# The tail of an attention block: when its output products are dealt out, where its turned sums lie, and which pair of the FFN comes second

## The chip, the cores and the metric

One core of one Trainium2 chip runs the whole program. The metric is device time in microseconds for one execution; the median of a few runs is given. Engines are named as in the profile: PE (TensorE), DVE (VectorE), ACT (ScalarE), POOL (GpSimd), SP (SyncE, which only issues transfers here).

## The reference

One sequence of 2048 rows, 576 columns; 32 heads of 18; an FFN of 4608.

```python
# A: x @ wqkv -> q, k, v; scores = q k^T * Dh**-0.5; p = softmax; o = p v; o @ wo
# B: g = x @ w_gate; u = x @ w_up; h = gelu_tanh(g) * u; h @ w_down
h  = x + A(layernorm(x), wqkv, wo)
h2 = h + B(layernorm(h), w_gate, w_up, w_down)      # what is returned
```

## The kernel before

Numbers are carried in pairs of fp16 (a high part and a remainder), so a product of two matrices is a sum of three products. Rows come in 16 tiles of 128, in NB=4 blocks of 512 (TPB=4 tiles each).

**Attention.** Eight groups of four heads by four query blocks give 32 blocks, n=0 to 31 (NS=32); g is the group and qc the query block. A block has 16 steps, kt, one for each tile of keys. In a step, two score products per pair of heads go to PSUM (`scores_pair`, L441), ScalarE takes their exponentials (L443), and one step later `weigh` (L447) multiplies them with the values into `acc`. The softmax needs the maximum over the keys of each query beforehand: a second run of score products (L400) whose maxima VectorE takes from PSUM (L403). This generator, `maxima`, runs 28 units ahead, at 16 units a block, so that it ends at n=30, kt=4. At the start of block n+1, `out_block` copies the sums of block n (L456, ScalarE, at kt=0), turns them by PE (L460) at kt=1, copies again (L462) and divides on GpSimd (L467 to L480), leaving fp16 pairs in `nat16`, the same memory as `nat`.

When all eight groups of a query block are done (n=28 to 31), its rows go through wo. `turn_o(b)` turns the four tiles of block b by a transposing DMA on SP (L538) into `OT`, which lies in region V. `wo_block(b)` then makes, for each of four tiles and two halves of columns, 14 products (L247) and adds x, fetched by a DMA into one of three buffers (L546), on VectorE (L551); row statistics follow (L159, L160), and after four tiles the reciprocal deviation (`rstd_of`, 13 short VectorE instructions).

**Toward the FFN.** The FFN multiplies 2x2 blocks by seven products instead of four (`quad`, seven products of seven matmuls, L889). For that, `pair_rows(p)` joins row tile i of an earlier and a later block: tiles of blocks 0 and 1 for p=0, of 2 and 3 for p=1. It normalises, forms sums and differences on VectorE and GpSimd (L585 to L589), casts them on ScalarE (L593), forms remainders on VectorE (L595, L596), and turns them by DMA on SP (L599) into `XP[p]`: XP[0] lies in region X, XP[1] in V. Weights come in 18 chunks; `split_mat` scales a chunk's gate or up matrix on ScalarE (L660), forms sums on GpSimd (L663, L666, L669), casts on ScalarE (L664, L667, L676, L685), and forms remainders on GpSimd (L673 to L688). The parts of even chunks lie in region A and of odd chunks in region W. `prepare` and `prepare_down` load and split chunk after chunk.

For chunk c and pair p the FFN runs `gate(c, p)` (one quad), `up(c, p)` (one quad, then the product with the gate on VectorE, a cast on ScalarE and a remainder on GpSimd, L932 to L934) and `down(c, p)` (96 matmuls, L247, added into `nat` on VectorE, L952).

**What sets the order.** Side work is written as Python generators. In the attention loop, `fill` holds products to be mixed in, `side` other work; each is advanced ("taken") twice a step, once for each `scores_pair`. In the FFN, `step(cost)` advances a clock in units, and each generator in `sides` goes on when its due time, raised by what it yields (3 if nothing), has come; a product of a quad counts 7 units, one of down 3.

The program has two parts that matter. The attention loop stands under a manual schedule for PE and POOL: their instructions keep the written order, while a compiler pass orders ACT, DVE and SP. The FFN stands under a manual schedule for every engine:

```python
    with tc.manual_schedule(engines={EngineType.PE, EngineType.Pool}):   # attention
...
    with tc.manual_schedule():                                           # FFN
        turn_o(NB - 1)
...
        ga = gate(0, 0, first_gate)
        for _ in wo_block(NB - 1):
            step(5)
        wait_for(1, "g")
        rows1 = begin(pair_rows(1))
        up(0, 0, ga, first_up)
```

There follow down(0,0), gate(0,1), up(0,1), gate(1,0), down(0,1), up(1,0) and so on. In the attention loop the blocks n=29, 30, 31 begin, at kt=1, with turn_o(0), turn_o(1), turn_o(2) and take up wo_block of the same number as `fill` at once, so that its products stand before the rest of the block's scores; prepare(0) and prepare_down(0) are `side` from n=28, kt=2, and pair_rows(0) is `side` from n=31, kt=1.

Of the kernel before, what the change touches and what calls it, by code (L numbers as in the profile page):

```python
# [30 lines left out]
def tile_block(  # L31
# [500 lines left out]

    OT = view(V, 0, (L // P, TB), F16)
    xbs = [view(V, 28544 + 4 * HALF * i, (HALF,)) for i in range(3)]

    def turn_o(b):
        for i in range(TPB):
            nc.sync.dma_start_transpose(OT[:, :, i * P : (i + 1) * P], nat16[:, b * TPB + i])  # L538

    def wo_block(b, each=False):  # L540

        for t in range(b * TPB, (b + 1) * TPB):
            for i in range(2):
                ws = slice(i * HALF, (i + 1) * HALF)
                xb = xbs[(2 * t + i) % 3]
                nc.sync.dma_start(xb, xv[:, t, ws])  # L546
                pt = next(m_ring)
                k = t - b * TPB
                run(accumulate(pt[:, :HALF], products(slice(k * P, (k + 1) * P), oh, ol, ws,
                                                      (OT[:, :NK], OT[:, NK], OT[:, NK + 1 :]))))  # L550
                nc.vector.scalar_tensor_tensor(nat[:, t, ws], pt[:, :HALF], u_o, xb,  # L551
                                               op0=ALU.mult, op1=ALU.add)
# [18 lines left out]
    def pair_rows(p):  # L571

        ys, z = rows[p]
        for v in ys:
            nc.gpsimd.memset(v[:, :, HALF + 64 : 3 * P], 0.0)
        for i in range(TPB):
            t1, t2 = 2 * p * TPB + i, (2 * p + 1) * TPB + i
            a, b = slice(0, HALF), slice(HALF, D)
            for k, t, h in ((6, t1, a), (3, t1, b)):
                nc.scalar.activation(z[:, k], nat[:, t, h], AF.Identity,  # L580
                                     scale=rs[:, t : t + 1], bias=nb[:, t : t + 1])
            normed(z[:, 0], nat[:, t2, b], t2)
            normed(z[:, 2], nat[:, t2, a], t2)
            yield
            nc.vector.tensor_add(z[:, 1], z[:, 6], z[:, 0])  # L585
            nc.gpsimd.tensor_add(z[:, 4], z[:, 6], z[:, 2])
            nc.vector.tensor_add(z[:, 5], z[:, 3], z[:, 0])
            nc.gpsimd.tensor_sub(z[:, 2], z[:, 2], z[:, 0])
            nc.vector.tensor_sub(z[:, 3], z[:, 3], z[:, 6])  # L589
            for j, k0, k1 in ((1, KA, 7), (0, 0, KA)):  # L590
                y, zz = ys[j], z[:, k0:k1]
                yield 5
                nc.scalar.copy(y[:, :, :HALF], zz)  # L593
                yield 5
                nc.vector.tensor_sub(y[:, :, 3 * P :], zz[:, :, : 2 * P], y[:, :, : 2 * P])  # L595
                nc.vector.tensor_sub(y[:, :, HALF : HALF + 32], zz[:, :, 2 * P :],  # L596
                                     y[:, :, 2 * P : HALF])
                nc.scalar.copy(y[:, :, HALF + 32 : HALF + 64], y[:, :, 2 * P : HALF])
# [3 lines left out]
            yield  # L602

# [34 lines left out]
    g1, _ = stage(W, 17920)  # L638
    sums1 = view(W, 8960, (3, 3, P), F32)
    sumsn = view(W, 28672, (3, 3, P), F32)  # L640
# [184 lines left out]
    def prepare_down(c):  # L825

        def after(k, last):
            while c and ghost[k] < last:
                yield

        if c == 1:
            yield from after("rows", 1)
        load_down(dn if c else d0, c, nc.sync)
        yield 48
        yield from after("d", 2 * (c - 1))
        yield from split_down(dn if c else d0, c)
        kept[c, "d"] = True
# [141 lines left out]
    side = iter(())  # L979
    with tc.manual_schedule(engines={EngineType.PE, EngineType.Pool}):  # L980
        for b in range(NB):
# [11 lines left out]
        for n in range(NS):  # L993
            g, qc = divmod(n, NB)
            acc = singles[3]
            for kt in range(NT):
                take(mxs)
                for pr in range(2):
                    scores_pair(n, kt, pr)
                    if g < NG - 1 or kt >= NT // 4:  # L1000
                        take(fill)
                    take(side)
                take(mxs)
                if prev is not None:
                    weigh(*prev)
# [28 lines left out]
        weigh(*prev)  # L1034
        for _ in out_block(prev[0], prev[2]):
            pass
        run(side)
        run(fill)
    with tc.manual_schedule():
# [19 lines left out]

        prev = (0, 0)  # L1060
        for c in range(NCH):
            for p in range(NPR):
                if (c, p) == (0, 0):
                    continue
                if (c, p) == (0, 1):
                    down(*prev)
                    while rows1 in sides:
                        step(1)
                    ghost["rows"] = 1
                wait_for(c, "g")  # L1070
                ga = gate(c, p)
                if (c, p) != (0, 1):
                    wait_for(prev[0], "d")
                    down(*prev)
                wait_for(c, "u")
# [29 lines left out]
```

## Time and profile before

| | |
|---|---|
| median of 3 runs | 2880.33 us (2877.4 to 2880.98) |
| profiled execution | 2879.98 us, span 2877.7 us |
| PE busy | 2686.3 us, 93% of the span |
| DVE busy | 2253.1 us, 78% |
| ACT busy | 1711.7 us, 59% |
| POOL busy | 1208.6 us, 42% |
| HBM | 40 GB/s over the span |

A row of the timeline reads: start, length, engine, line, operation, output from input, shapes, count; in brackets the idle time of the engine before it and what ended that. "x14" with a length is a run of fourteen. PEld is the load of weights into PE, SPq and POOLq are DMA issues. A row of the chain reads start, length, what.

### The profile page before, as it was taken

The numbers are of one execution on the slowest core, as the hardware profiler recorded it, in microseconds if no ns is written. First come the engines' busy times: TensorE is split into PE (matmuls) and PEld (weight loads), VectorE is DVE, ScalarE is ACT, GpSimd is POOL, SyncE is SP. The second block draws the span as 40 slices with busy tenths as digits, with TensorE's granted clock in tenths as the row PEclk, the third lists the DMA queues.
The fourth block names the chain that finished last, engine by engine and source line by source line (L and its number), as shares of the span: only waits on it lengthen the run. The fifth ranks groups of instructions, "written<-read, shape, count | busy, mean of one in ns | idle before, by whom it ended". The sixth has DMA issues, their size and how long they took to land.

```text
span 2877.7 us, 44734 instructions
## 1 busy us (share of the span) xinstructions
PE 2686.3 (93%) x16822; PEld 1122.5 (39%) x16822; DVE 2253.1 (78%) x3873; ACT 1711.7 (59%) x2144; POOL 1208.6 (42%) x1498
## 2 busy tenths in 40 slices
PE   6999899999999998999887869999999999999999
PEld 3532222222222222222132435555555555555555
DVE  7569899999999999999783477766667666667666
ACT  5217888888888888888766634444344444344431
POOL 0002475576557641121312336545544545555431
PEclk9999999999999999999899989999999999999999
DMA  8121221211212110000011641111111111111101
GB/s 216 55 74 46 73 66 43 63 63 34 59 51 75 59 32 13 1 26 3 5 34 42 124 87 39 42 31 31 31 41 40 31 31 31 31 35 38 31 1 66
DMA packets 146761, 136.27 MB, mean 47 GB/s; under 512 B 84720, under 2 KB 125808, under 8 KB 145392
## 3 DMA queue, kind: packets, MB, share of 16 engines
q1 hardware_dynamic: 134512, 92.99, 12.2%
q0 software_dynamic: 12032, 40.42, 4.4%
q8 instruction: 132, 2.16, 0.3%
q14 instruction: 85, 0.70, 0.1%
HBM read 100.27 MB, written 14.16 MB: 40 GB/s over the span
## 4 chain that ended last, share of the span: by engine, by line
PE 54%; DVE 35%; POOL 3%; issue 2%; ACT 2%; DMA 2%; SPq 0%; ACTq 0%; POOLq 0%; DVEq 0%
DVE mx L403 33%; PE acc L889 26%; PE acc L247 14%; PE pair L247 4%; PE bank L447 3%; PE bank L400 3%; PE bank L247 2%; ACT WK L443 1%; POOL rc L467 1%; PE bank L460 1%; PE pair L441 1%; DMA V<-nat 0%; DMA WK<-in_A_wqkv_dram 0%; DMA V<-in_A_x_dram 0%; POOL X L526 0%
## 5 line engine op out<-in xcount | busy, mean ns | idle before, releaser
L403 DVE TENSOR_REDUCE mx<-bank 128x1 f32<-128x512 f32 x2048 | 1275.2, 684 | 113.1 <-PE bank L400 111.9
L443 ACT ACTIVATE WK<-pair,p_ex_sc 128x1024 f32<-128x1024 f32 x1024 | 1086.1, 1114 | 223.3 <-PE pair L441 217.7
L447 PE MATMUL bank<-WK,V 128*32 128x512 f32 x4096 | 553.3, 612 | 0.1
L952 DVE SCALAR_TENSOR_TENSOR nat<-acc,p_w_dsc,nat 128x288 f32<-128x288 f32 x576 | 297.5, 518 | 118.6 <-PE acc L247 116.7
L247 PEld LDWEIGHTS <-WK 128*128 128x128 f16 x3456 | 339.1, 98 | 114.3 <-ACT WK L933 10.5
L467 POOL TENSOR_TENSOR rc<-WK,minus_one 128x16 f32<-128x16 f32 x32 | 93.8, 2931 | 650.3 <-ACT WK L462 650.3
L400 PE MATMUL bank<-W 54*128 54x512 f16 x1024 | 287.6, 386 | 42.1 <-DVE mx L403 12.8
L400 PE MATMUL bank<-A 54*128 54x512 f16 x1024 | 280.8, 381 | 37.8 <-DVE mx L403 12.6
L889 PEld LDWEIGHTS <-A 128*128 128x128 f16 x1764 | 172.7, 98 | 222.5 <-issue 18.4
L889 PEld LDWEIGHTS <-W 128*128 128x128 f16 x1764 | 171.8, 97 | 206.7 <-issue 0.2
L447 PEld LDWEIGHTS bank<-WK,V 128*32 128x32 f32 x4096 | 81.4, 108 | 413.7 <-issue 387.1
L247 PE MATMUL acc<-A,WK 128*128 128x288 f16 x1728 | 217.9, 288 | 15.4 <-ACT WK L933 8.3
L247 PE MATMUL acc<-W,WK 128*128 128x288 f16 x1728 | 216.5, 287 | 2.5 <-ACT WK L933 1.3
L889 PE MATMUL acc<-V,A 128*128 128x512 f16 x882 | 195.7, 382 | 8.4 <-DMA V<-WK 8.4
L889 PE MATMUL acc<-X,A 128*128 128x512 f16 x882 | 195.7, 381 | 4.1 <-ACT W L898 3.6
L889 PE MATMUL acc<-V,W 128*128 128x512 f16 x882 | 193.9, 379 | 0.0
L889 PE MATMUL acc<-X,W 128*128 128x512 f16 x882 | 193.8, 379 | 0.0
L934 POOL TENSOR_TENSOR WK<-ga,WK 128x512 f16<-128x512 f32 x74 | 91.2, 1232 | 226.9 <-ACT WK L933 182.4
L441 PE MATMUL pair<-W 56*128 56x512 f16 x1024 | 165.1, 384 | 20.8 <-ACT WK L443 20.3
L441 PE MATMUL pair<-A 56*128 56x512 f16 x1024 | 157.6, 379 | 5.7 <-DMA A<-mT 3.4
L400 PEld LDWEIGHTS <-W 54*128 54x128 f16 x1024 | 61.0, 93 | 231.1 <-issue 221.5
L663 POOL TENSOR_TENSOR W<-W 128x384 f32<-128x384 f32 x34 | 34.3, 1008 | 263.3 <-ACT W L660 222.6
(308 smaller groups left out, 3047.9 us busy)
## 6 DMA issues: line engine op xcount, KB each, us to landing
X<-in_B_w_down_dram POOLq DMA_DIRECT2D x9, 1152.0 KB, 5.5
WK<-in_B_w_down_dram SPq DMA_DIRECT2D x17, 576.0 KB
X<-in_B_w_gate_dram POOLq DMA_DIRECT2D x9, 1024.0 KB, 6.0
X<-in_B_w_up_dram POOLq DMA_DIRECT2D x9, 1024.0 KB, 5.8
W<-in_B_w_gate_dram SPq DMA_DIRECT2D x34, 256.0 KB
W<-in_B_w_up_dram SPq DMA_DIRECT2D x34, 256.0 KB
qk_hi<-qk SPq DMA_DIRECT2D x36, 128.0 KB
qk_lo<-qk SPq DMA_DIRECT2D x36, 128.0 KB
```

The lines of the kernel that those rows point to most:

```text
L247: nc.tensor.matmul(dst, a, b, start=(i == 0), stop=(i == len(pairs) - 1))
L400: nc.tensor.matmul(pms[j][:, :TB], Q[r, q0 : q0 + P], K[r, kc * TB : (kc + 1) * TB], start=True, stop=True)
L403: nc.vector.tensor_reduce(mx[:, t, 2 * pr + j, kc : kc + 1], pms[j][:, :TB], axis=AX.X, op=ALU.max)
L441: nc.tensor.matmul(pS[:, j, :TB], K[r, kt * P : (kt + 1) * P], Q[r, qc * TB : (qc + 1) * TB], start=True, stop=True)
L443: nc.scalar.activation(pes[(2 * kt + pr) % NPE], pS[:, :, :TB], AF.Exp, scale=ex_sc)
L447: nc.tensor.matmul(acc[32 * hh : 32 * hh + 32, :TB], Vg[n // NB][:, kt * G4 + hh * VC : kt * G4 + hh * VC + 32], pes[(2 * kt + hh // 2) % ...
L460: nc.tensor.transpose(pt[:, i * P : (i + 1) * P], oT[:, i * P : (i + 1) * P], id32)
L467: nc.gpsimd.tensor_tensor(rc, den, minus_one.to_broadcast([P, TPB * 4]), op=ALU.pow)
L663: nc.gpsimd.tensor_add(s167[:, 0], src[:, :3, f0], src[:, 3:, f1])
L889: nc.tensor.matmul(bank, w, x_, start=i == 0, stop=i == len(ps_) - 1)
L934: nc.gpsimd.tensor_sub(hl[:, f, b], r, hh[:, f, b])
L952: nc.vector.scalar_tensor_tensor(nat[:, t, ws], pt[:, :HALF], w_sc["dsc"], nat[:, t, ws], op0=ALU.mult, op1=ALU.add)
```

## The change

- `OT` gets several homes: OTs[0] in X, OTs[1] and OTs[2] in V, OTs[3] in W.
- `wo_block` yields after every second product, so that the caller deals them out.
- The attention loop keeps ACT in the written order too.
- Side work is paced: `slowly(it, cost)` advances a generator by cost units a take. prepare(0) and prepare_down(0) go at 3 units a take; pair_rows(0), now from n=31, kt=3, at 10. pair_rows yields more finely, and for p=0 two normalisations and a small copy go to VectorE.
- turn_o(0) and turn_o(1) stay at n=29 and n=30, kt=1; wo_block(0) begins after n=30, kt=4, at five takes a step, wo_block(1) at n=31, kt=0, at eight, with rstd for every tile. turn_o(2) moves to n=31, kt=11, and wo_block(2) behind the last weighing.
- The FFN starts with wo_block(3); then gate(0,0), up(0,0), gate(1,0), down(0,0), the rest of pair_rows(1), up(1,0), gate(0,1), down(1,0), up(0,1). The loop goes on with gate(1,1).
- Chunk 1's sums lie at W 28672 (wo's weights lie there before) instead of W 8960, and chunk 2's gate and down wait for one use more of the slots.

```diff
-    OT = view(V, 0, (L // P, TB), F16)
+    OTs = [view(X, 26112, (L // P, TB), F16)] + [view(V, 0, (L // P, TB), F16)] * (NB - 2)
+    OTs.append(view(W, 0, (L // P, TB), F16))
...
+                for j, (a, w) in enumerate(ps_):
+                    nc.tensor.matmul(pt[:, :HALF], a, w, start=j == 0, stop=j == len(ps_) - 1)
+                    if j % 2 and j < len(ps_) - 1:
+                        yield 1
...
             for k, t, h in ((6, t1, a), (3, t1, b)):
+                if p:
+                    nc.scalar.activation(z[:, k], nat[:, t, h], AF.Identity,
+                                         scale=rs[:, t : t + 1], bias=nb[:, t : t + 1])
+                else:
+                    normed(z[:, k], nat[:, t, h], t)
...
-    first_gate = ring([None] * 3 + [view(A, 22528, (TB,))])
+    first_gate = ring([None] * 3 + [view(A, 22528, (TB,)), view(W, 33280, (TB,), F32)])
...
-        sums = sums0 if first else [sums1, sumsn] if c == 1 else [sumsn] * 2
-        need = 2 * (c - 1)
+        sums = sums0 if first else [sumsn] * 2
+        need = 2 * (c - 1) + (c == 2)
...
-        yield from after("d", 2 * (c - 1))
+        while (c, "u") not in kept:
+            yield
+        yield from after("d", 2 * (c - 1) + (c == 2))
...
+    def slowly(it, cost):
+        due = 0
+        for r in it:
+            due += r or 3
+            while due > 0:
+                due -= cost
+                yield
...
-    with tc.manual_schedule(engines={EngineType.PE, EngineType.Pool}):
+    with tc.manual_schedule(engines={EngineType.PE, EngineType.Pool, EngineType.Activation}):
...
-                    if g < NG - 1 or kt >= NT // 4:
+                    if g < NG - 1:
                         take(fill)
                     take(side)
                 take(mxs)
+                if g == NG - 1:
+                    take(fill, 5 if qc == NB - 2 else 8)
...
-                    if n > NS - NB:
-                        run(fill)
+                    if n == NS - NB + 1 or n == NS - 2:
                         turn_o(qc - 1)
-                        fill = wo_block(qc - 1)
-                        if qc == 3:
-                            run(side)
-                            side = pair_rows(0)
+                if n == NS - 2 and kt == 4:
+                    fill = wo_block(0)
+                if n == NS - 1 and kt == 0:
+                    run(fill)
+                    fill = wo_block(1, each=True)
+                if n == NS - 1 and kt == 11:
+                    run(fill)
+                    turn_o(NB - 2)
+                if n == NS - 1 and kt == 3:
+                    run(side)
+                    side = slowly(pair_rows(0), 10)
...
-                    side = chain(prepare(0), prepare_down(0))
+                    side = slowly(chain(prepare(0), prepare_down(0)), 3)
...
         weigh(*prev)
-        for _ in out_block(prev[0], prev[2]):
-            pass
+        ob = out_block(prev[0], prev[2])
+        next(ob)
+        fill = wo_block(NB - 2)
+        take(side, 4)
+        take(fill, 8)
+        run(ob)
+        for _ in fill:
+            take(side)
         run(side)
-        run(fill)
     with tc.manual_schedule():
         turn_o(NB - 1)
...
+        for u in wo_block(NB - 1):
+            step(1)
         begin(rest)
         begin(down_preparer())
+        rows1 = begin(pair_rows(1))
         ga = gate(0, 0, first_gate)
-        for _ in wo_block(NB - 1):
-            step(5)
+        up(0, 0, ga, first_up)
         wait_for(1, "g")
-        rows1 = begin(pair_rows(1))
-        up(0, 0, ga, first_up)
-        prev = (0, 0)
+        ga = gate(1, 0, first_gate)
+        down(0, 0)
+        while rows1 in sides:
+            step(1)
+        ghost["rows"] = 1
+        wait_for(1, "u")
+        up(1, 0, ga)
+        ga = gate(0, 1)
+        wait_for(1, "d")
+        down(1, 0)
+        up(0, 1, ga)
+        prev = (0, 1)
```

More of the change, by code (lines that the diff above doesn't have):

```diff
@@ L537, in turn_o @@
         for i in range(TPB):
-            nc.sync.dma_start_transpose(OT[:, :, i * P : (i + 1) * P], nat16[:, b * TPB + i])
+            nc.sync.dma_start_transpose(OTs[b][:, :, i * P : (i + 1) * P], nat16[:, b * TPB + i])
     def wo_block(b, each=False):
+        OT = OTs[b]
+        xs = (OT[:, :NK], OT[:, NK], OT[:, NK + 1 :])
         for t in range(b * TPB, (b + 1) * TPB):
@@ L548, in wo_block @@
                 k = t - b * TPB
[L549 to L550 removed]
+                ps_ = products(slice(k * P, (k + 1) * P), oh, ol, ws, xs)
+                for j, (a, w) in enumerate(ps_):
+                    nc.tensor.matmul(pt[:, :HALF], a, w, start=j == 0, stop=j == len(ps_) - 1)
+                    if j % 2 and j < len(ps_) - 1:
+                        yield 1
                 nc.vector.scalar_tensor_tensor(nat[:, t, ws], pt[:, :HALF], u_o, xb,
@@ L1049, in wait_for @@
                 step(1)
+        for u in wo_block(NB - 1):
+            step(1)
         begin(rest)
         begin(down_preparer())
+        rows1 = begin(pair_rows(1))
         ga = gate(0, 0, first_gate)
-        for _ in wo_block(NB - 1):
-            step(5)
+        up(0, 0, ga, first_up)
         wait_for(1, "g")
-        rows1 = begin(pair_rows(1))
-        up(0, 0, ga, first_up)
-        prev = (0, 0)
+        ga = gate(1, 0, first_gate)
[10 more added lines that the diff above has]
+        prev = (0, 1)
         for c in range(NCH):
             for p in range(NPR):
-                if (c, p) == (0, 0):
+                if c == 0 or (c, p) == (1, 0):
                     continue
[L1065 to L1069, printed above, removed]
                 wait_for(c, "g")
                 ga = gate(c, p)
-                if (c, p) != (0, 1):
-                    wait_for(prev[0], "d")
-                    down(*prev)
+                wait_for(prev[0], "d")
+                down(*prev)
                 wait_for(c, "u")
```

18 lines of the change are left out of this document (10 added, 8 removed).

## The prediction, before the run

> **What bounds the kernel now.** I read the page first (span, busy times, the 40 slices), then stage windows, then the timeline where a stage has gaps, and the chain that ended last.
>
> ```profile
> span 2877.7 us, 44734 instructions
> PE 2686.3 (93%) x16822; PEld 1122.5 (39%) x16822; DVE 2253.1 (78%) x3873; ACT 1711.7 (59%) x2144; POOL 1208.6 (42%) x1498
> PE   6999899999999998999887869999999999999999
> ```
>
> PE is full in most slices; the dents lie in slices 20 to 24, where attention hands over to the FFN. The windows cut that region at the copies that close the blocks n (L456), and at the milestones behind them. One block before, n=28, 29, 30, 31, then gate(0,0) with wo_block(3), then the stretch up to gate(0,1), then two steady iterations:
>
> ```profile
> 1357.80:1398.80 41.00, 38.36 (x265) 9.44 (x262) 39.57 (x66) 36.26 (x40) 6.09 (x10) 1.00 0.04 12
> 1398.80:1453.30 54.50, 44.44 (x265) 9.62 (x262) 40.39 (x67) 38.28 (x40) 26.78 (x39) 0.81 0.00 1
> 1453.30:1515.20 61.90, 54.71 (x375) 20.03 (x373) 48.00 (x98) 36.08 (x38) 8.94 (x14) 0.94 0.17 39
> 1515.20:1569.70 54.50, 46.73 (x323) 17.84 (x320) 20.61 (x52) 34.56 (x37) 7.22 (x12) 0.94 0.20 45
> 1569.70:1628.40 58.70, 45.98 (x302) 17.37 (x301) 26.08 (x64) 45.26 (x57) 15.69 (x21) 0.91 0.58 111
> 1628.40:1657.60 29.20, 25.47 (x166) 16.12 (x167) 11.33 (x24) 9.65 (x14) 14.05 (x22) 1.00 0.46 109
> 1657.60:1712.80 55.20, 27.83 (x148) 15.25 (x146) 44.55 (x82) 21.76 (x35) 26.67 (x28) 0.79 0.48 85
> 1746.80:1812.90 66.10, 66.10 (x391) 37.86 (x389) 47.09 (x74) 28.03 (x44) 39.71 (x45) 1.00 0.15 45
> ```
>
> Columns are stage, length, then busy PE, PEld, DVE, ACT, POOL, granted clock, DMA. The block before is DVE's: 39.57 of 41. The four blocks after it take 229.6 together (54.5 + 61.9 + 54.5 + 58.7) with no engine full. The last two need no maxima after their first quarter. At 1657.6 DVE is the limit (44.55 of 55.2) and PE half idle; later PE is full and nothing else matters. So the span moves by the arrival at the first full PE stretch, corrected for work done before it. The copy that closes n=31, and four of the stalls:
>
> ```profile
> 1628.44 0.59 ACT L456 COPY WK<-bank 128x512 f32<-128x512 f32 x1 [1.15 <-PE bank L447]
> 1411.95 1.15 ACT L676 CAST A<-X 128x1152 f16<-128x1152 f32 x1 [2.56 <-POOL X L669]
> 1424.30 1.15 ACT L676 CAST A<-X 128x1152 f16<-128x1152 f32 x1 [4.96 <-POOL X L669]
> 1465.94 3.54 PE L247 MATMUL bank<-W,V 128*128 128x288 f16 x14 [4.55 <-DMA V<-nat]
> 1582.05 3.54 PE L247 MATMUL bank<-W,V 128*128 128x288 f16 x14 [5.67 <-DMA V<-nat]
> ```
>
> In n=28 ScalarE sits at a split's cast until GpSimd has made the sums, with the exps behind it. In n=29 and n=31 PE sits at the first product of a wo_block until the turned sums land, then runs it at half pace (3.54 for 14).
>
> **The change, part by part.**
>
> ```profile
> 1370.73 0.51 ACT L664 CAST A<-X 128x384 f16<-128x384 f32 x1
> 1416.49 0.83 ACT L685 CAST A<-X 128x768 f16<-128x768 f32 x1 [1.36 <-POOL X L678]
> 1686.45 0.93 ACT L660 ACTIVATE W<-W,p_w_u 128x768 f32<-128x768 f32 x1
> 1551.60 11.17 ACT L443 ACTIVATE WK<-pair,p_ex_sc 128x1024 f32<-128x1024 f32 x11 [2.02 <-PE pair L441]
> 1551.11 0.61 PE L441 MATMUL pair<-W 56*128 56x512 f16 x4
> 1551.64 1.07 PE L447 MATMUL bank<-WK,V 128*32 128x512 f32 x8
> 1480.12 1.88 PE L247 MATMUL bank<-W,V 128*128 128x288 f16 x14
> 1591.66 0.91 ACT L593 CAST V<-V 128x864 f16<-128x864 f32 x1 [0.21 <-issue]
> 1593.65 1.15 ACT L593 CAST V<-V 128x1152 f16<-128x1152 f32 x1
> ```
>
> *n=28 and n=29: prepare(0) paced, ScalarE in program order, no products.* A split's ACT work is 2 x 0.93 + 2 x 0.51 + 1.15 + 0.83 = 4.9. Paced at 3 units a take, its 72 units fill 24 takes, 12 of a block's 16 steps, so GpSimd has its sums ready before the casts. 36.26 + 4.9 = 41.2 is the block's length: I take 42 each, with 41 (cover holds) and 47 (half the excess of n=28 stays) as ends. wo_block(0) is gone from n=29; its turn by DMA stays on SP at kt=1 and now has a block to land.
>
> *n=30.* Up to kt=4 the step is DVE's, 41/16 = 2.56. From kt=5 five takes carry ten products: 10 x 1.88/14 = 1.3. PE per step: scores 0.53 (1551.11 to 1551.64), weighing 1.0, products 1.3, so 2.85, over ScalarE's 11.17/11 x 2 = 2.03. 5 x 2.56 + 11 x 2.85 = 44.2, with a wait for the last maxima 45 (43 to 48).
>
> *n=31.* wo_block(1) at eight takes: 16 products, 2.1, a step 3.65, for kt=1 to 8, 29.2. The other eight are ScalarE's: 2.03 plus pair_rows(0), two casts a row tile (0.91 + 1.15) over 2.9 steps, 2.75; 22.0. With the last exp and weighing, 54 (48 to 60). Two normalisations and one small copy a row tile go from ACT to DVE, which has no maxima then: nothing. rstd is formed per tile, 13 short DVE instructions instead of a fourth of them: hidden by the same idle DVE. turn_o(2) leaves kt=1 for kt=11; behind it on SP queue only transposes of pair_rows(0) and x loads.
>
> Sum 42 + 42 + 45 + 54 = 183 against 229.6: 46.6 less.
>
> *Between attention and gate(0,0).*
>
> ```profile
> 1632.26 2.91 POOL L467 TENSOR_TENSOR rc<-WK,minus_one 128x16 f32<-128x16 f32 x1
> 1637.60 0.67 POOL L480 TENSOR_TENSOR nat<-o,nat 128x256 f16<-128x256 f32 x1
> 1638.29 5.64 SPq L538 DMA_TRANSPOSE V<-nat  x4
> 1641.56 5.32 PE L247 MATMUL acc<-W,V 128*128 128x288 f16 x42 [0.51 <-DMA V<-nat]
> 1655.88 1.88 PE L247 MATMUL acc<-W,V 128*128 128x288 f16 x14 [1.72 <-DVE nat L551]
> 1655.31 0.94 DVE L551 SCALAR_TENSOR_TENSOR nat<-acc,u_o,V 128x288 f32<-128x288 f32 x2 [4.45 <-DMA V<-in_A_x_dram]
> ```
>
> Before, gate(0,0) covered the chain copy, transposes, GpSimd (1632.26 to 1638.27), turn (3.3 to the first product). Now wo_block(2) covers it, from OTs[2] in V while OTs[3] in W is being filled: 112 products, 8 x 1.88 = 15. The chain is as long (13.1 from L456 to 1641.56), so PE hardly waits. wo_block(3) took 1641.56 to 1657.76, 16.2, x loads in the way; its step(1) with no side begun puts no weight load into SP between the x loads. 33 with the ends' copies (29 if x loads vanish, 40 if they queue behind the turns of block 3). Before: 29.2.
>
> *From there to gate(0,1).*
>
> ```profile
> 1707.88 4.84 DMA V<-WK
> 1712.77 34.08 PE acc L889 x147
> 1746.85 11.76 PE acc L247 x96
> 1758.61 21.33 PE acc L889 x98
> 1633.58 0.69 DVE L897 TENSOR_TENSOR ga<-ga,acc 128x512 f32<-128x512 f32 x1 [17.73 <-PE acc L889]
> L589 DVE TENSOR_TENSOR V<-V 128x288 f32<-128x288 f32 x4 | 2.7, 678 | 0.1
> L589 DVE TENSOR_TENSOR WK<-WK 128x288 f32<-128x288 f32 x4 | 4.3, 1086 | 0.1
> ```
>
> PE now has gate(0,0), up(0,0), gate(1,0), down(0,0) and up(1,0) for this time: four quads of 21.33/2 and 11.76, 54.4. DVE has what filled 44.55 before (pair_rows(1), up, down, the last rstd) and two gates more, 8 x 0.69 = 5.5 each: 55.6. Before, it ran those 44.55 in the 50.3 from 1657.6 to the last turn at 1707.88, 89%; so 62.5, then that turn, 4.84. up(1,0) keeps its temporaries where pair_rows(1) has z and y, so its first ACT copy is a new wait for that turn; behind it stand ACT's other copies, and PE has four banks ahead and then stops. From the turn's end some 4.5 pass (three products, 21.33/14 each) until gate(0,1): 72.
>
> ```profile
> 1409.01 0.99 POOL L663 TENSOR_TENSOR X<-X 128x384 f32<-128x384 f32 x1
> 1421.38 0.99 POOL L663 TENSOR_TENSOR X<-X 128x384 f32<-128x384 f32 x1
> ```
>
> Also new: chunk 1's gate split. Its sums now lie on wo's weights and its parts on OTs[3], so GpSimd and ACT can't begin it before wo_block(3) ends; behind it on GpSimd stand pair_rows(1)'s sums and up's remainders. The 12.4 of a split (from one L663 to the next) fit ahead of gate(1,0), due after 21.3. The up load follows on SP behind turns of pair_rows(1).
>
> The two L589 rows (four each, in 1398 to 1629 and in 1659 to 1712) show a price: 0.41 more a piece where a split ran beside. The old stage holds one split already; for the second, five such lines a row tile make 0 to 8, and I take 3, since it covers a fifth of the stage. So 75 (62 if DVE hides behind PE's 54.4 but for the turn; 95 if each queue waits for the next).
>
> The Trainium skill, "SBUF — State Buffer", section "Who interferes with whom", says that a VectorE instruction with two SBUF inputs and a GpSimd instruction that reads SBUF exclude each other for the whole instruction. The rows agree. By that rule taken to its end all 12.4 of the second split's GpSimd time would be added, 9 more than my 3, and the sum would be 2845, inside the forecast's own range.
>
> *The rest.* Chunk 2's gate waits for the third gate instead of the second and its down split for up: PE has down, up, gate, down, up between (2 x 11.76 + 3 x 10.7 = 55.5), against 12.4 of GpSimd: nothing.
>
> **Sum.** 183 + 33 + 75 = 291, against 229.6 + 84.3 = 313.9 from 1398.84 to 1712.77. In it PE has also done gate(1,0) and up(1,0), 21.3, which before came after: 291 - 21.3 - 313.9 = -44. The profiled execution took 2879.98 (0.35 under the median 2880.33): 2836. All low ends together give 2809, all high ends 2882.
>
> **Rivals.**
> *The hand-over eats more.* PE works in bursts at DVE's pace. Its clock was 0.79 in that stage before; 54.4 / 0.79 = 69 still hides under 75. At half clock, as in the 14 products of 3.54 against 1.88, it is 109, 34 more: 2870; with queues waiting for each other, 95: 2856. For it: every engine there runs in written order. Against: the PE work is twice as dense. The Trainium skill, "TensorE: Matmul & The Clock Gate", section "What's actually happening", has the clock halved after an idle window of some 3.4 us; the rows of 3.54, each after a longer wait, agree.
> *The dealing doesn't fill.* If casts still stand before exps and n=28 and n=29 stay 54.5, 25 of the 44 are gone: 2861. If all four do, 218 in place of 183: 2871, and with one high end behind it no change. Against: the pacing puts 6 us between sum and cast.
> *Slower: ScalarE's written order costs in all 27 earlier blocks.* A copy that waits (L456 for the weighing) now always holds the exps. From 44/27 = 1.6 us a block it decides; at 2.5 the time is 2903. Against: a block has 41 - 36.26 = 4.7 of ACT slack, and L456 stands between exps already.
>
> **How the numbers follow.** Forecast (2814 to 2852) 0.60, hand-over eats more (2852 to 2871) 0.18, dealing doesn't fill 0.10, half of it within 0.2%, slower 0.07, better than 2814 0.05. 0.2% (6 us) is about what a measurement can tell. Faster 0.87, same 0.05, slower 0.08. The range 2814 to 2866 leaves two tenths out.
>
> **What would show it.** The L456 copies some 42, 42, 45 and 54 apart; no PE wait on V<-nat inside a block; exps with no idle on POOL X; wo_block(2) directly behind the last weighing; gate(0,1) starting 108 us after the last L456, DVE over 80% busy till then. It is wrong if a block before n=28 lengthens, if a block of the four stays above 54, or if PE waits over 10 us for chunk 1's parts.

## The result, and the profile after

| kernel | median, us | all runs, us | ratio to before, 95% interval |
|---|---|---|---|
| before | 2880.09 | 2877.4 to 2880.98 | |
| after | 2842.58 | 2841.24 to 2848.32 | 0.9875 [0.9858, 0.9892] |

The change takes 37.5 us off. The forecast was 2836 with a range of 2814 to 2866. The profiled execution took 2842.06.

From the page of the kernel after: the span, the busy times, and PE's 40 slices.

```profile
span 2840.3 us, 44778 instructions
PE 2674.8 (94%) x16822; PEld 1120.7 (39%) x16822; DVE 2265.0 (80%) x3928; ACT 1703.1 (60%) x2128; POOL 1209.3 (43%) x1498
PE   6999899999999999999989789999999999999999
```

PE has the same number of matmuls. The five slices 20 to 24 at the hand-over read 8 8 7 8 6 before and 9 8 9 7 8 now. Of the 37.4 by which the span is shorter, 25.9 is idle time of PE; the other 11.5 (2686.3 - 2674.8) is busy time, since the same matmuls run faster on average. Next the windows of the kernel after, cut at its own milestones: the block before, n=28 to n=31, from the last L456 copy to the end of wo_block(3), from there to the last three products of up(1,0), then one further on. Columns as in the prediction.

```profile
1356.80:1397.50 40.70, 38.27 (x265) 9.32 (x262) 39.55 (x66) 34.75 (x36) 6.08 (x10) 1.00 0.04 12
1397.50:1441.40 43.90, 38.57 (x268) 9.30 (x265) 41.17 (x68) 40.47 (x45) 19.02 (x28) 1.00 0.00 1
1441.40:1482.80 41.40, 37.48 (x261) 8.96 (x258) 38.39 (x63) 36.75 (x40) 16.81 (x26) 1.00 0.16 30
1482.80:1531.30 48.50, 44.48 (x323) 16.01 (x320) 18.25 (x37) 36.08 (x38) 6.84 (x11) 0.96 0.21 47
1531.30:1582.80 51.50, 42.86 (x304) 15.91 (x304) 40.96 (x136) 41.34 (x44) 13.55 (x18) 0.97 0.65 126
1582.80:1619.10 36.30, 30.58 (x229) 23.42 (x228) 17.13 (x49) 0.95 (x2) 5.57 (x9) 0.91 0.51 105
1619.10:1689.00 69.90, 54.38 (x272) 27.40 (x270) 53.62 (x98) 35.06 (x57) 38.78 (x46) 0.93 0.47 92
1784.00:1810.00 26.00, 23.86 (x120) 11.57 (x119) 17.23 (x24) 14.07 (x22) 17.34 (x20) 1.00 0.01 2
```

The four blocks take 185.2 in place of 229.6. In n=28 and n=29 DVE and ACT fill the block again; in n=30 PE has 44.48 of 48.5. From the chain of the work that ended last, the hand-over into the first full PE stretch, and two rows of the timeline that take its 70 matmuls apart:

```profile
1683.34 4.92 DMA V<-WK
1689.00 17.29 PE acc L912 x70
1718.06 21.21 PE acc L912 x98
```

```profile
1689.00 6.69 PE L912 MATMUL acc<-X,W 128*128 128x512 f16 x21 [4.97 <-ACT WK L918]
1695.53 10.77 PE L912 MATMUL acc<-V,A 128*128 128x512 f16 x49
```

The 70 matmuls are the last three products of up(1,0), which run slowly after a wait, and the seven of gate(0,1), which begins at 1695.5. From there to the end of the span the kernel before took 1164.9 (2877.7 - 1712.77) and this one 1144.8 (2840.3 - 1695.5).

So the account is: the start of n=28 is 1.3 earlier (1397.52 against 1398.84), the way from there to gate(0,1) is 15.9 shorter (298.0 against 313.9), and the part behind gate(0,1) is 20.1 shorter, mainly because gate(1,0) and up(1,0), 21.3, are already done. Together 37.3; the spans differ by 37.4.

### The profile page after: what moved, and what is told of

Its sections match the earlier page's. It is cut to its first block, busy times and chain, and to the rows that moved or that the text cites. A ratio compares the mean times of both kernels' runs of the same rounds, so it can differ in the third digit from the quotient of the medians.

```text
span 2840.3 us, 44778 instructions
## 1 busy us (share of the span) xinstructions
PE 2674.8 (94%) x16822; PEld 1120.7 (39%) x16822; DVE 2265.0 (80%) x3928; ACT 1703.1 (60%) x2128; POOL 1209.3 (43%) x1498
## 4 chain that ended last, share of the span: by engine, by line
PE 54%; DVE 37%; ACT 3%; issue 2%; POOL 2%; DMA 1%; SPq 1%; ACTq 0%; DVEq 0%; POOLq 0%
DVE mx L403 34%; PE acc L912 25%; PE acc L247 15%; PE pair L247 4%; PE bank L447 4%; PE bank L400 3%; ACT WK L443 1%; PE bank L247 1%; PE bank L554 1%; PE bank L460 1%; PE acc L554 1%; PE pair L441 1%; POOL rc L467 0%; DMA WK<-in_A_wqkv_dram 0%; POOL X L526 0%
## 5 line engine op out<-in xcount | busy, mean ns | idle before, releaser
L400 PE MATMUL bank<-A 54*128 54x512 f16 x1024 | 282.3, 382 | 38.1 <-DVE mx L403 13.5
L912 PEld LDWEIGHTS <-W 128*128 128x128 f16 x1764 | 172.2, 98 | 218.4 <-issue 13.8
L912 PEld LDWEIGHTS <-A 128*128 128x128 f16 x1764 | 172.2, 98 | 211.7 <-issue 6.4
L912 PE MATMUL acc<-X,W 128*128 128x512 f16 x882 | 196.6, 381 | 8.7 <-ACT WK L918 5.0
L912 PE MATMUL acc<-X,A 128*128 128x512 f16 x882 | 195.7, 381 | 3.6 <-DVE ga L932 3.0
L912 PE MATMUL acc<-V,W 128*128 128x512 f16 x882 | 194.0, 379 | 0.5 <-ACT ga L918 0.5
L912 PE MATMUL acc<-V,A 128*128 128x512 f16 x882 | 193.8, 379 | 0.0
L441 PE MATMUL pair<-W 56*128 56x512 f16 x1024 | 157.9, 378 | 11.2 <-ACT WK L443 10.7
L400 PEld LDWEIGHTS <-A 54*128 54x128 f16 x1024 | 60.4, 93 | 215.0 <-issue 206.7
```

What stands on the lines that cost most here:

```text
L400: nc.tensor.matmul(pms[j][:, :TB], Q[r, q0 : q0 + P], K[r, kc * TB : (kc + 1) * TB], start=True, stop=True)
L441: nc.tensor.matmul(pS[:, j, :TB], K[r, kt * P : (kt + 1) * P], Q[r, qc * TB : (qc + 1) * TB], start=True, stop=True)
L912: nc.tensor.matmul(bank, w, x_, start=i == 0, stop=i == len(ps_) - 1)
```

## The experiments

Line numbers here are those of the kernel after: L554 the products of wo_block, L557 their sum with x, L549 the load of x, L539 the turn, L912 the quads, L613 the turns of pair_rows, L596/L599 its sums on GpSimd, L607/L609 its remainders, L676 to L701 the sums and remainders of a split. A kernel of an experiment may be off by one or two. The kernel before, timed again beside each group of experiments, had medians of 2878.77 to 2879.65, so a difference of a microsecond or two between two kernels is not to be read. Lengths of n=28 to n=31, from the L456 copies:

| kernel | n=28 | n=29 | n=30 | n=31 | sum | median time |
|---|---|---|---|---|---|---|
| before | 54.5 | 61.9 | 54.5 | 58.8 | 229.6 | 2880.09 |
| after | 43.9 | 41.4 | 48.6 | 51.4 | 185.2 | 2842.58 |
| ACT not in written order | 46.7 | 47.5 | 49.7 | 54.7 | 198.6 | 2853.9 |
| prepare(0) not paced | 44.1 | 42.9 | 48.9 | 51.4 | 187.3 | 2846.36 |
| before, with order and pacing | 45.1 | 62.6 | 55.8 | 61.6 | 225.1 | 2876.98 |
| after, products early | 43.9 | 69.7 | 57.8 | 57.2 | 228.5 | 2877.75 |

### What shortens the four blocks

**ScalarE's order left to the compiler.**

```diff
-    with tc.manual_schedule(engines={EngineType.PE, EngineType.Pool, EngineType.Activation}):
+    with tc.manual_schedule(engines={EngineType.PE, EngineType.Pool}):
```

> The changed kernel, but ScalarE is left to the compiler pass again in attention, as before; all else stays. Theory (the pacing of the splits is what keeps their casts from standing before the exps, the written order matters less): n=28 grows by some 5, time 2847. Rival (the written order is what does it): n=28 goes back to some 54, time 2853 or more. Rival (it does nothing): 2843.

Measured: 2853.9 (2849.56 to 2856.53), ratio to before 0.9913 [0.9898, 0.9927]. The four blocks are 13.4 longer, and every one of them is. With the rest of the change in place, the written order is worth some 11 us of the 37.5. But n=28 takes 46.7, far from the 54 of the rival: with pacing alone, ScalarE's casts wait 4.0 in n=28 for GpSimd's sums (2.6 and 1.4), against 10.2 (7.5 and 2.7) in the kernel before.

**prepare(0) taken at full pace.**

```diff
-                    side = slowly(chain(prepare(0), prepare_down(0)), 3)
+                    side = chain(prepare(0), prepare_down(0))
```

> The changed kernel, but chunk 0's splits are not paced: one take, one piece of the split, as before; ScalarE keeps the written order. Theory: GpSimd falls behind, the split's casts wait on ScalarE with the exps behind them, n=28 is 52 or more in place of 43.9 and n=29 is near 41: time 2851. Rival (the written order suffices): 2843.

Measured: 2846.36 (2842.88 to 2848.9), 0.9884 [0.9867, 0.99]. The blocks are 2.1 longer in sum, the median 3.8, with overlapping runs. The prediction put the stall of n=28 down to GpSimd's sums and its cure to the pacing. With ScalarE in written order the pacing is not needed for it: paced or not, n=28 takes 44, and no cast waits for GpSimd there. Together with the experiment before this shows two cures, either of which removes most of the stall: from the 54.5 with neither, pacing alone gives 46.7 and the written order alone 44.1.

**Both of these in the kernel before.**

```diff
+    def slowly(it, cost): ...                 # as in the kernel after
-    with tc.manual_schedule(engines={EngineType.PE, EngineType.Pool}):
+    with tc.manual_schedule(engines={EngineType.PE, EngineType.Pool, EngineType.Activation}):
-                    side = chain(prepare(0), prepare_down(0))
+                    side = slowly(chain(prepare(0), prepare_down(0)), 3)
```

> The kernel before, with two things of the change only: ScalarE in the written order in attention, and chunk 0's splits paced at 3 units a take. Theory (n=28's excess is the casts that wait for GpSimd): n=28 falls from 54.5 to 43 or 44, the other blocks keep 62, 54.5 and 58.7: 2869. Rival (written order costs in the earlier blocks, or the wait only moves to n=29): 2880 or more.

Measured: 2876.98 (2874.64 to 2880.89), 0.9993 [0.9983, 1.0002]: no difference that shows, where 2869 was expected. n=28 falls by 9.4, nearly as in the kernel after, but n=30 and n=31 rise by 1.3 and 2.8. Alone, these two edits bring nothing that the runs can tell from zero.

**The products early again.** Everything as after, but wo_block(0), (1) and (2) are taken up at kt=1 of n=29, 30 and 31, right behind each turn, as before, and dealt at seven and five takes a step; the homes of the turned sums stay.

```diff
-                    if n == NS - NB + 1 or n == NS - 2:
-                        turn_o(qc - 1)
-                if n == NS - 2 and kt == 4:
-                    fill = wo_block(0)
...
+                    if n > NS - NB:
+                        run(fill)
+                        turn_o(qc - 1)
+                        fill = wo_block(qc - 1)
...
-                    take(fill, 5 if qc == NB - 2 else 8)
+                    take(fill, 7 if qc < NB - 1 else 5)
...
-        fill = wo_block(NB - 2)
```

> The changed kernel, but wo_block(0), (1), (2) are taken up again at n=29, 30, 31, kt=1, right behind their turn, seven takes a step (one group of 14 products) in n=29 and n=30 and five in n=31; written order, pacing, homes and pair order stay. Theory (where the products stand is what made these blocks long: PE waits for the turn, and products compete with the maxima): n=29 some 58, n=30 some 52, n=31 some 58, while the last wo_block(2) leaves the tail and its cover goes too: 2868. Rival (written order did it all; the products only move): 2843 to 2848.

Measured: 2877.75 (2875.64 to 2880.17), 0.9998 [0.9989, 1.0007]. The whole gain is gone: the four blocks are 43.3 longer, and the way from the last L456 copy to the end of wo_block(3) is 8.7 shorter (27.7 for 36.4), as wo_block(2) no longer stands there. n=28, which has no products, stays at 43.9. The window of that kernel over n=29, and two rows of its timeline there:

```profile
1445.00:1515.00 70.00, 54.98 (x376) 20.41 (x369) 48.49 (x98) 37.11 (x39) 16.01 (x25) 0.93 0.15 35
```

```profile
1456.88 3.54 PE L554 MATMUL bank<-W,X 128*128 128x288 f16 x14 [9.02 <-DMA X<-nat]
1463.40 1.88 PE L554 MATMUL bank<-W,X 128*128 128x288 f16 x14 [0.23 <-DVE mx L403]
```

Its waits from 1400 to 1625 (in total, times, longest), and ScalarE's of the kernel after from 1397 to 1583:

```profile
ACT WK L443 <- PE pair L441: 71.8, 33, 13.7
PE bank L554 <- DMA V<-nat: 17.9, 2, 9.3
```

```profile
ACT WK L443 <- PE pair L441: 24.1, 37, 1.6
```

PE, in written order, stands at the first product for 9.02 until the turned sums have landed, and then runs 14 matmuls in 3.54; the scores stand behind it, so the exps wait: 71.8 against 24.1, 13.7 at the longest against 1.6. These are the 3.54s of the prediction's rows of before. That the moment of the products decides is thus shown: with the rest in place, 35 of the 37.5 us hang on it. The wait for the turned sums is not all of that. It is 26.9 in three places (9.02 and the 17.9 above). In n=29, which is 28.3 longer, it is only 9.0; from the first group of 14 products to the eighth there pass 35.9 (1456.88 to 1492.79), seven steps, where seven steps of n=29 in the kernel after take 18.1 (7 x 41.4 / 16). There the products stand among the maxima, with which they share three banks of PSUM, and before the groups PE waits for a maximum on VectorE (the second row). A version with the products late but dealt among maxima, which would price the two apart, was not tried.

### What follows attention

**The order of the pairs as before**, with all else as after: gate(0,1) follows down(0,0), and gate(1,0), up(1,0) come in the loop. What chunk 2's gate and down wait for goes back with it.

```diff
-        wait_for(1, "g")
-        ga = gate(1, 0, first_gate)
         down(0, 0)
...
-        wait_for(1, "u")
-        up(1, 0, ga)
         ga = gate(0, 1)
-        wait_for(1, "d")
-        down(1, 0)
         up(0, 1, ga)
```

> The changed kernel with the pair order of before: gate(0,0), up(0,0), down(0,0), then gate(0,1) once pair_rows(1) is through, up(0,1), and chunk 1 after that. Theory (VectorE and the last turn set that stretch, not what PE has to do in it): VectorE has 5.5 less in it, so gate(0,1) starts 61 after wo_block(3) in place of 75, with 21.3 of PE work still to come: 7 slower, 2850. Rival (the order carries the gain, PE starves without chunk 1's first pair): 20 or more slower, 2863.

Measured: 2860.85 (2860.1 to 2865.84), 0.9942 [0.9927, 0.9957]: 18.3 slower than after. Windows of it from the end of wo_block(3) to gate(0,1), and the row of gate(0,1):

```profile
1626.10:1658.00 31.90, 23.52 (x100) 9.88 (x98) 26.45 (x53) 17.34 (x29) 19.34 (x25) 0.91 0.28 61
1658.00:1694.70 36.70, 14.31 (x97) 10.03 (x96) 24.18 (x37) 13.18 (x21) 19.94 (x22) 0.69 0.59 118
```

```profile
1694.68 19.55 PE L912 MATMUL acc<-V,A 128*128 128x512 f16 x77 [20.55 <-DMA V<-WK]
```

The time lies nearer to the rival's 2863 than to the 2850 of the theory, which had the stretch fall by 14. Without the two quads the stretch takes 68.6, with them 76.4. So 21.3 us of PE work ride along for 7.8. From the end of wo_block(3) to the end of the span the profiles have 1238.0 (2864.1 - 1626.1) and, after, 1221.2 (2840.3 - 1619.1): the order of the pairs is worth 16.8 there. (This profile is of the slowest of the four runs, by 5 us; what else it is longer by lies ahead of the stretch.) DVE is busy 50.6 of the 68.6, idle 18.0: the stretch does not shrink in proportion to its work.

**Less VectorE work in that stretch.** pair_rows(1) leaves its remainders out, so the products with them are missing from the output.

```diff
-                nc.vector.tensor_sub(y[:, :, 3 * P :], zz[:, :, : 2 * P], y[:, :, : 2 * P])
+                if not p:
+                    nc.vector.tensor_sub(y[:, :, 3 * P :], zz[:, :, : 2 * P], y[:, :, : 2 * P])
...                                            # the second one likewise; memset wider for p=1
```

> The changed kernel with less VectorE work in the stretch between wo_block(3) and gate(0,1): pair_rows(1) leaves out its two subtractions that form the remainders (that part of XP[1] is set to zero, so the remainder products of pair 1 are missing from the output). It takes some 13.5 us of VectorE's 53.6 out of the 69.9 us from the end of wo_block(3) to the 70-matmul run. If VectorE sets that stretch, as the prediction had it (55.6 of work at 89%), it falls by 10 to 13, to 57 to 60, and the time from 2842.6 to about 2831. If the hand-offs set it (VectorE or GpSimd sum, ScalarE cast, next), with VectorE 77% busy, the cast still waits for the sums, and the stretch falls by 4 or less, time 2838 to 2842. If PE's 54.4 sets it: no change.

Measured: 2837.52 (2831.95 to 2841.11), 0.9852 [0.9837, 0.9867]. The window from the end of wo_block(3) to the last three products of up(1,0), in this kernel:

```profile
1620.70:1682.20 61.50, 50.90 (x273) 26.35 (x271) 43.57 (x82) 34.56 (x57) 38.67 (x46) 0.99 0.51 106
```

The 16 instructions left out were 10.05 of DVE (53.62 - 43.57), not 13.5, and the stretch fell by 8.4 (69.9 to 61.5). Neither bound of the expectation was met by the stretch: most of what VectorE loses, the stretch loses. The time is less clear: the median is only 5.1 lower than after's, and the runs spread over 9 us. VectorE's idle part hardly moved: 16.3 after, 17.9 here, 18.0 with the old order. The largest single wait in it, after and here, is the one for the last turn, which goes by way of ScalarE's first copy of up(1,0):

```profile
DVE WK L920 <- ACT WK L918: 7.4, 1, 7.4
DVE WK L922 <- ACT WK L920: 8.6, 1, 8.6
```

So the stretch is VectorE's work, that last turn, and some 9 us of hand-offs in which VectorE waits for a cast or a product (4.9 in the fastest kernel, below, where the split is out of the way).

**Five x buffers instead of three.** The rows of the kernel after from the last block to wo_block(3):

```profile
1582.75 0.58 ACT L456 COPY WK<-bank 128x512 f32<-128x512 f32 x1 [0.33 <-PE bank L447]
1586.72 0.52 DVE L557 SCALAR_TENSOR_TENSOR nat<-bank,u_o,V 128x288 f32<-128x288 f32 x1 [1.14 <-PE bank L554]
1591.12 0.67 POOL L480 TENSOR_TENSOR nat<-o,nat 128x256 f16<-128x256 f32 x1
1591.81 1.30 SPq L539 DMA_TRANSPOSE W<-nat  x1
1593.20 0.52 SPq L549 DMA_DIRECT2D V<-in_A_x_dram  x1
1595.95 0.52 DVE L557 SCALAR_TENSOR_TENSOR nat<-bank,u_o,V 128x288 f32<-128x288 f32 x1 [4.55 <-DMA V<-in_A_x_dram]
1602.85 16.25 PE L554 MATMUL acc<-W 128*128 128x288 f16 x112 [4.45 <-DVE nat L557]
```

The turn of block 3 stands on SP between the last loads of x for wo_block(2). wo_block(2)'s second sum sets a buffer free at 1587.24, but the load into it goes out only at 1593.20: on SP it stands behind the first transpose of the turn, which waits for the division until 1591.79 and then holds the queue for 1.30. DVE waits 4.55 for that load, and wo_block(3) starts 20.1 after the L456 copy.

```diff
-    xbs = [view(V, 28544 + 4 * HALF * i, (HALF,)) for i in range(3)]
+    xbs = [view(V, 28544 + 4 * HALF * i, (HALF,)) for i in range(5)]
-                xb = xbs[(2 * t + i) % 3]
+                xb = xbs[(2 * t + i) % 5]
```

> The changed kernel with five buffers for x instead of three. Theory (wo_block(2) stood 4.55 at an x load that went out late behind a turn on SP, so wo_block(3) began 5 late): wo_block(3) starts 16 after the last L456 in place of 20, time 2838. Rival (the turn of block 3 sets that start anyway): 2842.

Measured: 2838.33 (2835.62 to 2838.74), 0.9857 [0.9842, 0.9872]. wo_block(3) starts 15.9 after the copy (1585.8 to 1601.66). As expected.

**Block 3's turned sums in V, chunk 1's gate split begun before wo_block(3).** Then the split need not wait until wo_block(3) has read W.

```diff
-    OTs.append(view(W, 0, (L // P, TB), F16))
+    OTs.append(view(V, 0, (L // P, TB), F16))
+    sums1 = view(W, 8960, (3, 3, P), F32)
...
-        sums = sums0 if first else [sumsn] * 2
+        sums = sums0 if first else [sums1, sumsn] if c == 1 else [sumsn] * 2
...
+        begin(rest)
         for u in wo_block(NB - 1):
             step(1)
-        begin(rest)
```

> The changed kernel with two edits: the turned sums of block 3 lie in V like those of blocks 1 and 2, and chunk 1's gate sums lie at W 8960 again, so that its split can start while wo_block(3) runs. Theory (a split beside pair_rows(1) makes VectorE's two-input instructions longer and holds ScalarE): 12 us of GpSimd leave the stretch behind wo_block(3), which falls from 75 to some 71; the turn waits only for the tiles of wo_block(2) that it overwrites, which are done: 2838. Rival (the stretch is set by the hand-offs of pair_rows(1), not by what else runs): 2842. Rival (the second home was needed: the turns wait for wo_block(2)): 2847.

> Five buffers for x and the home in V with the early split together. Theory: the gains add, 2834. Rival: one takes the other's place, 2838.

Measured: 2844.34 (2841.79 to 2847.51) with three x buffers and 2840.75 (2839.48 to 2842.73) with five; 0.9877 [0.986, 0.9893] and 0.9868 [0.9853, 0.9883]. The stretch behind wo_block(3) falls from 69.9 to 63.9 and 63.4, and yet no time is won, since wo_block(3) now starts 25.2 and 22.4 after the copy. The timeline of the second:

```profile
1585.93 1.00 POOL L677 TENSOR_TENSOR W<-W 128x384 f32<-128x384 f32 x1 [5.77 <-ACT W L674]
1594.62 2.92 POOL L467 TENSOR_TENSOR rc<-WK,minus_one 128x16 f32<-128x16 f32 x1
1603.21 0.67 POOL L480 TENSOR_TENSOR nat<-o,nat 128x256 f16<-128x256 f32 x1
1608.58 3.70 PE L554 MATMUL acc<-W,V 128*128 128x288 f16 x17 [8.18 <-DVE nat L557]
```

GpSimd takes the split first, and the last division, on which the turn waits, stands behind and between its instructions.

**The same, with the split's sums where the last block's copies lie**, so that it can't come before the division.

```diff
-    sums1 = view(W, 8960, (3, 3, P), F32)
+    sums1 = view(WK, 16384, (3, 3, P), F32)
```

> Five x buffers, the turned sums of block 3 in V and chunk 1's gate split begun before wo_block(3), as in the run before, but with that split's sums at WK 16384, where the copies of the last out_block lie: so GpSimd does the last division first and then the split. If the lost 6 us at the start of wo_block(3) in that run were GpSimd's 9 us of split ahead of the division, wo_block(3) now starts 16 us after the last L456 copy (22.4 there), the stretch behind it stays at 64, and the time is 2838 - 6 = 2832. Rival: the split then stands against pair_rows(1) again, stretch back to 68 to 70 and time 2837 to 2840, as with five x buffers alone.

Measured: 2831.76 (2830.8 to 2832.84), 0.9834 [0.9819, 0.9849], the fastest of all, 10.8 under the kernel after. Its timeline, and the window of the stretch:

```profile
1594.78 0.68 POOL L480 TENSOR_TENSOR nat<-o,nat 128x256 f16<-128x256 f32 x1
1600.76 5.30 PE L554 MATMUL acc<-W,V 128*128 128x288 f16 x42 [0.97 <-DVE nat L557]
```

```profile
1615.90:1679.60 63.70, 52.60 (x273) 26.81 (x272) 51.35 (x98) 31.46 (x51) 25.95 (x28) 0.97 0.46 89
```

Against the L456 copy (1586.18 above, 1585.57 here) the division ends 7.8 earlier, wo_block(3) starts 15.2 after the copy, and the stretch stays short. Both gains now add up, 4.9 and 6.2 in the profiles. So it was GpSimd's order that had eaten them.

### A wait that the written order made at the start

The blocks n=2 and n=3 together take 95.1 in the kernel after, 92.1 before, and 90.8 with all as after but ScalarE's order left to the compiler. The kernel before with order and pacing has 95.2, so it is the written order. A row of the waits of the kernel after, 300 to 410, names the place: prepare_wo's first scaled copy stands on DVE's scale, the exps behind it.

```profile
ACT W L525 <- DVE p_s_wo L144: 5.4, 1, 5.4
```

So I let prepare_wo wait, once on the fastest kernel and once on that with five x buffers.

```diff
         s_o = pow2(e_o, -1, 268, "s_wo")
+        for _ in range(8):
+            yield
```

> The same, and prepare_wo waits eight takes between forming the scale (DVE) and the first scaled copy on ScalarE. In the written order that copy stood 5.4 us on the scale with the exps behind it, and the blocks from n=1 to n=3 took 95.1 in place of 92.1. With the takes between, 3 us less than the kernel without it: about 2829. Rival: the copy wait moves elsewhere and nothing is won: 2832.

> The changed kernel with five x buffers and the eight takes in prepare_wo, without the moves of the turned sums and the split: 2838.3 - 3 = 2835. If prepare_wo's wait is not a loss of its own: 2838.

Measured: 2840.96 (2838.04 to 2846.03), 0.9869 [0.9852, 0.9885], and 2846.4 (2844.46 to 2849.22), 0.9885 [0.9871, 0.99]: 9.2 and 8.1 slower than without. In n=2 and n=3 nothing is won either (95.05 against 94.5 without), and n=8 takes 47.9 for 41.9. From the waits of the first, 300 to 410, and of the fastest kernel in the same window:

```profile
PE bank L768 <- POOL X L760: 6.3, 1, 6.3
```

```profile
PE bank L766 <- POOL X L758: 1.2, 1, 1.2
```

The wait on the scale (5.0 in the fastest kernel) is gone, and n=2 is 5.0 shorter; but n=3 is 5.5 longer. The scan of the weights, which follows prepare_wo in the same chain, has moved too: its product on PE now waits 6.3 for GpSimd, with the scores behind it (and 5.6 once more near 600). My expectation counted one wait and not what is queued behind the delay. That the scan's shift is the cause is read from these rows and not tried by itself, and it is not all: of the 8.6 between the profiles of the first kernel and of the fastest, 2.9 arise behind the last L456 copy (1247.3 from there to the end, against 1244.4), long after the scan, and why is open.

The worths of the parts, each read with the rest in place (11 for the written order, 35 for the moment of the products, 18 for the order of the pairs), add up to more than the 37.5 of the whole: they need one another.

## Why the prediction was right, step by step

| step | predicted | measured after |
|---|---|---|
| n=28, 29, 30, 31 | 42, 42, 45, 54: 183 | 43.9, 41.4, 48.6, 51.4: 185.2 |
| last L456 to end of wo_block(3) | 33 | 36.4 |
| end of wo_block(3) to gate(0,1) | 75 | 76.4 |
| behind gate(0,1), against before | -21.3 | -20.1 |
| time | 2836 | 2842.58 |

*The blocks.* The sum holds, and no exp waits on GpSimd any longer. The reason given for n=28 holds in half: pacing alone removes 7.8 of its excess, but the written order alone removes 10.4, so that in this kernel the pacing adds next to nothing. n=31 is 2.6 short and n=30 3.6 long; that the two nearly cancel in the sum is luck. n=30 lost its time at a place that the prediction named only as "a wait for the last maxima":

```profile
1486.25 2.93 POOL L467 TENSOR_TENSOR rc<-WK,minus_one 128x16 f32<-128x16 f32 x1 [19.19 <-ACT WK L462]
1493.58 0.22 POOL L414 TENSOR_TENSOR mm<-m,mm 128x16 f16<-128x16 f32 x1
1493.86 0.23 PE L418 MATMUL bank<-id,mm 128*32 128x128 f16 x1 [3.30 <-POOL mm L414]
```

The last maxima's scaling stands on GpSimd behind the division of block 29, and PE waits 3.30 for it, where the prediction had allowed 0.8 (45 against 44.2). An edit that moves it was not tried. One sign that the prediction had named as telling against it did come: a block before n=28 lengthened, n=2 (52.4 in place of 47.2), as told above.

*From the last copy to the end of wo_block(3).* The sum went by wo_block(3)'s own x loads; the loads that came late were wo_block(2)'s last, behind the turn on SP. The high end of 40, "if they queue behind the turns of block 3", names just this. The step was mis-sized by 3.4; five buffers gave 4.3 back in time.

*To gate(0,1).* The sum of 75 is 1.4 short, and its parts are nearly right. Up to the last turn it had 62.5 + 3 = 65.5; the last transpose goes out 64.2 after wo_block(3) (1619.10 to 1683.34). VectorE's work in that is smaller than foretold (53.6, against 55.6 and 3 for contention) and so is its share (83%, against 89%), so the two errors cancel. From there to PE's start 5.7 pass in place of 4.84, and up(1,0)'s last three products take 6.5 in place of 4.5, as PE is slow after the wait. Up to gate(0,1) VectorE is busy 60.0 of 76.4, 78%: the sign of over 80% was just missed. The rival that each queue waits for the next was the right picture for the some 9 us of hand-offs, at a smaller price. The second split's 3 us was for contention alone. In the fastest kernel, where that split is out of the stretch, the stretch is 6.2 shorter: VectorE's busy time is 2.3 less for the same 98 instructions (53.62 to 51.35), and the other 3.9 were waits. A row tile's sums on GpSimd stood behind the split, which itself stood on a cast:

```profile
1625.38 1.25 POOL L596 TENSOR_TENSOR WK<-WK 128x288 f32<-128x288 f32 x1 [3.15 <-DVE WK L188]
1639.13 1.16 POOL L700 TENSOR_TENSOR W<-W 128x512 f16<-128x512 f32 x1 [3.30 <-ACT W L698]
1641.36 0.80 POOL L596 TENSOR_TENSOR WK<-WK 128x288 f32<-128x288 f32 x1
```

16.0 pass from the first tile's sum to the second's; in the fastest kernel, 12.3. The Trainium skill, "SBUF — State Buffer", section "Who interferes with whom", has a VectorE instruction with two SBUF inputs and a reading GpSimd instruction contend. Taken to its end it gave 12.4; the 2.3 of busy time that the run shows is the part that such contention can account for.

*Behind gate(0,1).* PE is idle for 9.4 there, against 6.5 before. 2.14 of the 2.9 more fall into the window from 1784 to 1810, where PE is busy 23.86 of 26.00:

```profile
1807.17 1.30 DVE L709 SCALAR_TENSOR_TENSOR W<-WK,p_w_d,W 128x576 f16<-128x576 f32 x1 [2.16 <-ACT W L707]
1809.55 0.90 PE L247 MATMUL acc<-A,WK 128*128 128x288 f16 x6 [2.14 <-DVE nat L975]
```

So "nothing" was right for chunk 2's gate, for which PE doesn't wait. The loss is one block of work later: VectorE stands at a remainder of the next down split (into W, so of an odd chunk) until ScalarE has cast it, and down's products wait for the sums behind it on VectorE. Against this stands a gain of some 2 that the prediction didn't count: before, gate(0,1) itself ran slowly behind the wait for the last turn (its and up(0,1)'s 98 matmuls took 23.48, 98 later ones 21.33).

*The rivals.* "The hand-over eats more" did not come about as a whole: PE's clock was 0.93 there, and PE waited some 5 for the last turn (4.97). "The dealing doesn't fill" was wrong for after, and it is exactly what the experiment with early products shows. "ScalarE's written order costs in the earlier blocks" did not come about at its size: from the first L456 to n=28's start the kernel after takes 1128.6 (1397.52 - 268.88), the kernel before 1129.7 (1398.84 - 269.18) and the kernel after without the written order 1127.1 (1399.66 - 272.59). So against the same kernel without it the written order costs 1.6 us over these 27 blocks, where 44 would have decided, though n=2 and n=3 alone lose 3 to 4. It earned 11 us in the tail.

## What to carry to other kernels

Deal filler work out only where its inputs have long landed, and not where it shares buffers with a stream that is itself the limit: in a written order all that stands behind a filler waits with it, and here the early place cost 35 us. Before a side chain is moved or begun earlier, write down for each queue that it uses (GpSimd and SP too) which instruction of the main path will stand behind it; an address that overlaps with that instruction's data is a cheap way to hold it back. A stretch that an engine fills to 77% may still be set by that engine: here 10.05 us less of its work took 8.4 off. Count its work, its hand-offs and the last transfer behind it as terms of their own; a share that comes out right can hide two errors.

## What the runs showed of the hardware

A transposing DMA of one 128-row tile of block 3's sums holds SP's queue for 1.3 to 1.5 us, the larger of pair_rows(1)'s two parts (L613, V<-WK) for 3.0 to 3.1. A load of 0.5, queued behind a transpose that itself waits for its data, went out 6.0 after its buffer was free (1593.20 against 1587.24); that cost DVE 4.55 and PE 4.45. And a short wait is paid twice: the 21 matmuls of up(1,0), which PE began after 4.97 of waiting for the last turn, took 6.69, against 21.21/98 x 21 = 4.5 in the full stretch.
